# Attention and MLP on one core: the low halves of three quarters of the second weight split on another engine, and a new written order

## The chip, the cores and the metric

The kernel runs on one core of a Trainium2 chip. The metric is the device time of one execution in microseconds (us), the median over several runs; lower is better. The engines are TensorE (PE, matmuls; PEld its weight loads), VectorE (DVE), ScalarE (ACT), GpSimd (POOL) and SyncE (SP, which only issues DMAs). Each works through its own queue of instructions in order and waits for others by semaphores.

## The reference

```python
# x (8, 8, 512, 64), state (8, 8, 32, 64): per batch and head
scores = x @ state.T / 8;  a  = softmax(scores);   xread = a @ state
scores2 = state @ x.T / 8; a2 = softmax(scores2);  sread = a2 @ x
y = concatenate([xread, sread], axis=2)     # (8, 8, 544, 64) -> (8, 544, 512)
mu, var = mean(y), var(y)                   # over the last axis
yn = (y - mu) / sqrt(var + 1e-6) * g_ln
out = y + maximum(yn @ w_ch1, 0) @ w_ch2    # w_ch1 512 x 2048, w_ch2 2048 x 512
```

All in float32.

## The kernel before

**Split products.** A float32 operand is written as two float16 tiles, a high half hi = fp16(t*s) and a low half lo = fp16(t*s - hi), with a scale s per operand, and a product is three fp16 products (TERMS: hi*hi, hi*lo, lo*hi). `split` makes the two: ScalarE writes hi by a scaled copy, then the engine that it is given (VectorE unless told otherwise) writes lo by one scalar_tensor_tensor, (t * s) - hi.

**Units and stages.** The 2048 hidden columns are four units of 512 (u = 0 to 3). For each unit `weights1` loads its piece of the first weight, takes a power-of-two scale from its sum of squares (on PE, L670) and splits it (`w1c`); `weights2` does the same for the second weight. `weights2` ends in a loop over two halves of 128x1024: ScalarE writes `w2h` hi, VectorE `w2h` lo. The loaded weight's tile is named `sums` or `raw`, by the buffer that it lies in, so the same step reads `w2h<-sums` in some units and `w2h<-raw` in others. `sums_of_weights(u)` then forms four differences and sums of the quarters of the second weight in place on GpSimd (128x512 each, `sums<-sums`, `raw<-raw`), and splits them into four 128x512 pairs. They serve a product with fewer multiplications (a Strassen scheme in `products`, L895 and L953) for the later batches.

**The first batch** goes a plainer way: `first_products` (L799) multiplies a unit's first weight, ScalarE copies the result out of PSUM into one of three `strip` buffers and writes `hid` hi, GpSimd writes `hid` lo; `second_products_by_unit` (L813) multiplies by `w2h[u]` into PSUM `acc`, ScalarE copies it scaled to `part` (two buffers), and a DMA issued from GpSimd's queue adds it to the residual in memory (`xr<-part`). This happens while the weights are still coming in. From about 160 us on all products are those of L895 and L953, batch after batch.

**The order.** Nothing is scheduled by a compiler: every step is recorded in a stream by `do` (L187, which is why most rows of the trace bear that line), and a table of text, `PLAN`, gives the order in which `issue` takes items from the streams ("10:4-5" is steps 4 to 5 of stream 10). Streams 5, 10, 15 and 23 are `weights2` of units 0 to 3; 17 to 19 and 28 are `sums_of_weights`; 6, 11, 16 and 24 the second products. `WARM` dummy matmuls on a tile of ones (`half<-ones`, stream 177) are put by the same table where PE would wait.

Of the kernel before, what the change touches and what calls it, by code (L numbers as in the profile page):

```python
# [160 lines left out]
)  # L161
WARM = 135


class Later:
# [36 lines left out]
def moe_attention(ctx: ExitStack, tc: tile.TileContext, x, state, g_ln, w1, w2, out):  # L202
# [507 lines left out]
    def weights2(u):  # L710
# [17 lines left out]
        for fh in range(2):  # L728
            q = slice(2 * fh, 2 * fh + 2)
            yield from split(w[:, 0, q], w[:, 1, q], t.rearrange("p (q e) -> p q e", q=4)[:, q], s)  # L730
# [347 lines left out]
```

## Time and profile before

| what | value |
|---|---|
| median of 3 runs | 631.17 us (630.79 to 631.66) |
| the profiled execution | 632.65 us, its span 630.5 us |
| granted TensorE clock | 0.998 |
| PE busy | 614.7 us, 97% |
| VectorE busy | 488.7 us, 78% |
| ScalarE busy | 375.3 us, 60% |
| GpSimd busy | 242.5 us, 38% |
| dummy matmuls | 135 |

A row of the trace's timeline has start, length, engine, line, operation, out<-in tile, shapes and, in brackets, how long the engine had been idle before it and what released it. A row of groups has the count, then busy us and mean ns of one, then idle time before and its releasers. Names are the program's tile names without numbers, shapes are partitions x elements.

### The profile page before, as it was taken

What the parts mean: (1) busy time and instruction counts of PE and PEld (TensorE: products, weight loads), DVE (VectorE), ACT (ScalarE), POOL (GpSimd) and SP (SyncE); (2) the same over time, 40 slices, a digit from 0 to 9 for tenths busy, and PEclk for the clock granted to TensorE, in tenths of its full rate; (3) what the DMA queues carried; (4) which work ended last, traced back from release to release, by engine and by line L of the source; (5) the groups of instructions that cost most, each with busy time, mean ns of one, the idle gap of its engine ahead of it and who ended that gap; (6) DMA issues with size and microseconds to landing.
All of it is one profiled execution on the core that took longest, in us unless ns stands there. A gap on an engine that the chain in (4) does not pass through costs nothing.

```text
span 630.5 us, 16626 instructions
## 1 busy us (share of the span) xinstructions
PE 614.7 (97%) x6906; PEld 483.5 (77%) x6906; DVE 488.7 (78%) x1095; ACT 375.3 (60%) x678; POOL 242.5 (38%) x205
## 2 busy tenths in 40 slices
PE   9998998999999999999999999999999999999995
PEld 4355645558888888888888888888878888888884
DVE  4999998898697888688778785889578787564454
ACT  4998988868464844575376454736474544443241
POOL 0011656772262345324433532336224352424132
PEclk9999999999999999999999999999999999999999
DMA  8985293441534143534311246143504025201002
GB/s 289 412 232 191 84 206 68 102 120 43 130 113 120 24 96 68 155 52 132 89 34 39 43 102 156 43 102 50 143 2 77 2 63 145 69 11 25 35 1 68
DMA packets 85355, 62.02 MB, mean 98 GB/s; under 512 B 64608, under 2 KB 77408, under 8 KB 84832
## 3 DMA queue, kind: packets, MB, share of 16 engines
q1 hardware_dynamic: 83008, 57.00, 33.6%
q0 software_dynamic: 864, 3.15, 2.6%
q8 instruction: 54, 0.88, 0.6%
q10 hardware_dynamic: 1408, 0.82, 0.5%
q14 instruction: 21, 0.17, 0.1%
HBM read 28.05 MB, written 9.44 MB: 59 GB/s over the span
## 4 chain that ended last, share of the span: by engine, by line
PE 79%; DVE 13%; ACT 3%; DMA 2%; POOL 1%; issue 1%; DVEq 0%; ACTq 0%
PE acc L953 43%; PE half L895 23%; PE half L905 3%; PE banks L753 3%; DMA xr<-part 2%; PE acc L813 2%; DVE raw L187 2%; DVE x L187 1%; PE half L187 1%; DVE sums L187 1%; DVE w1c L187 1%; PE banks L590 1%; DVE w2h L187 1%; PE banks L472 1%; PE banks L565 1%
## 5 line engine op out<-in xcount | busy, mean ns | idle before, releaser
L953 PEld LDWEIGHTS <-xs 128*128 128x128 f16 x2520 | 244.0, 98 | 34.4 <-issue 6.0
L187 POOL TENSOR_TENSOR xs<-rs,xs 128x512 f16<-128x512 f32 x120 | 144.3, 1212 | 276.4 <-ACT xs L187 195.2
L953 PE MATMUL acc<-w2h,xs 128*128 128x256 f16 x1440 | 182.4, 273 | 0.0
L895 PE MATMUL half<-ea,matrix 128*128 128x256 f16 x1344 | 160.0, 273 | 0.1
L895 PEld LDWEIGHTS <-matrix 128*128 128x128 f16 x1344 | 129.4, 98 | 22.7 <-issue 5.1
L953 PE MATMUL acc<-sums,xs 128*128 128x256 f16 x1080 | 140.7, 273 | 0.0
L187 DVE SCALAR_TENSOR_TENSOR rs<-half,rs 128x256 f32<-128x256 f32 x224 | 90.0, 418 | 43.1 <-ACT rs L187 14.6
L187 ACT ACTIVATE xs<-rs 128x512 f16<-128x512 f32 (+1 forms) x128 | 77.3, 618 | 75.2 <-DVE rs L187 69.0
L187 ACT ACTIVATE xs<-half 128x256 f16<-128x256 f32 (+1 forms) x112 | 53.0, 485 | 58.3 <-PE half L895 30.7
L187 DVE SCALAR_TENSOR_TENSOR xs<-half,xs 128x256 f16<-128x256 f32 (+1 forms) x112 | 60.4, 548 | 24.2 <-ACT xs L187 23.0
L187 POOL TENSOR_TENSOR ts<-ts,mA 128x1024 f32<-128x1024 f32 (+1 forms) x16 | 29.1, 1818 | 55.4 <-DVE mA L187 32.4
L187 ACT ACTIVATE rs<-half 128x256 f32<-128x256 f32 x56 | 21.3, 381 | 39.5 <-PE half L895 32.8
L187 DVE SCALAR_TENSOR_TENSOR matrix<-banks,hs,matrix 128x1024 f16<-128x1024 f32 x28 | 35.8, 1279 | 11.4 <-ACT matrix L187 11.1
L813 PE MATMUL acc<-w2h,hid 128*128 128x512 f16 x192 | 43.2, 379 | 0.2 <-ACT strip L187 0.2
L187 DVE TENSOR_TENSOR strip<-acc,strip 128x256 f32<-128x256 f32 (+1 forms) x60 | 32.9, 549 | 9.1 <-PE acc L953 5.2
L813 PEld LDWEIGHTS <-hid 128*128 128x128 f16 x192 | 18.4, 98 | 23.9 <-issue 3.3
L187 PE MATMUL half<-ones 128*128 128x512 bf16 x135 | 34.9, 402 | 1.1 <-DVE part_mean L358 1.1
L187 ACT ACTIVATE matrix<-banks,hs 128x1024 f16<-128x1024 f32 x28 | 31.1, 1109 | 8.1 <-PE banks L753 8.0
L187 POOL TENSOR_TENSOR hid<-strip,hid 128x512 f16<-128x512 f32 x16 | 21.8, 1369 | 23.2 <-ACT hid L187 23.1
L187 PEld LDWEIGHTS <-ones 128*128 128x128 bf16 x135 | 13.0, 102 | 17.8 <-issue 5.8
L187 DVE SCALAR_TENSOR_TENSOR x<-x_f,x_s,x 128x512 f16<-128x512 f32 x32 | 24.8, 801 | 1.0 <-ACT x L187 0.9
L799 PE MATMUL acc<-ea,matrix 128*128 128x256 f16 x192 | 22.8, 272 | 2.5 <-DVE w1c L187 1.2
(152 smaller groups left out, 756.0 us busy)
## 6 DMA issues: line engine op xcount, KB each, us to landing
raw<-in_moe_w_ch_dram SPq DMA_DIRECT2D x11, 1024.0 KB, 8.5
out_dram<-xr SPq DMA_DIRECT2D x16, 512.0 KB, 3.3
x_f<-in_x_dram SPq DMA_DIRECT2D x14, 512.0 KB, 5.3
sums<-in_moe_w_ch_dram SPq DMA_DIRECT2D x5, 1024.0 KB, 8.0
ek<-ea SPq DMA_DIRECT2D x56, 64.0 KB, 2.0
ek<-ek SPq DMA_DIRECT2D x7, 512.0 KB, 4.2
xr<-part POOLq DMA_DIRECT2D x6, 512.0 KB, 4.6
s_r<-in_state_dram SPq DMA_DIRECT2D x28, 64.0 KB, 3.7
```

What stands on the lines that cost most here:

```text
L187: return lambda: f(*map(now, args), **{k: now(v) for k, v in kw.items()})
L472: nc.tensor.matmul(o[32 * j:32 * j + 32], lhsT=state_of(b, sT, g, j, a), rhs=xT[:, 2 * j + g].rearrange("p c t -> p (c t)"), start=a == 0, ...
L565: nc.tensor.matmul(o[32 * j:32 * j + 32, g], lhsT=ebT[:, e, g, c, 32 * j:32 * j + 32], rhs=xv[:, 2 * j + g, c, i], start=c == 0 and n == 0 ...
L590: nc.tensor.matmul(px[:, c, D * h:D * h + D], lhsT=ek[:, h % 2, h // 2, (2 * t + c) * P:(2 * t + c + 1) * P], rhs=sk[:, h], start=True, st ...
L753: nc.tensor.matmul(ps[g][32 * j:32 * j + 32], lhsT=state_of(b, sT, g, j, i)[r], rhs=w[r, k, j], start=n == 0, stop=n == 2, skip_group_chec ...
L799: nc.tensor.matmul(o[:, 256 * f:256 * f + 256], lhsT=m[:, g, i, P * (q + f):P * (q + f) + P], rhs=ea[:, s, k, g], start=f == 0 and g == 0 ...
L813: nc.tensor.matmul(po, lhsT=hid[:, i, q, c * P:(c + 1) * P], rhs=w[:, j, q], start=first and q == 0 and n == 0, stop=last and q == 3 and n ...
L895: nc.tensor.matmul(ps[:, 256 * q:256 * q + 256], lhsT=m[:, h, i, P * (2 * k + q):P * (2 * k + q) + P], rhs=ea[:, 0, j, h, 256 * g:256 * g ...
L905: nc.tensor.matmul(ps[:, 256 * q:256 * q + 256].rearrange("p (t n) -> p t n", t=2), lhsT=w[:, i, j, fs], rhs=xsT[:, :, x, j], start=q == 0 ...
L953: nc.tensor.matmul(po[o], lhsT=y[:, n, i, o] if o < 2 else x[:, o - 2, n, i], rhs=v[j], start=u == 0 and n == 0 and k == 0 and o in (2, 1, ...
```

## The change

In `weights2` the units 1 to 3 no longer use `split`. ScalarE first multiplies the loaded half by its scale in place (`raw<-raw,of_weights` or `sums<-sums,of_weights`, 128x1024), then copies it to hi without a scale, and GpSimd subtracts hi from it to give lo (`tensor_tensor`). `sums_of_weights` of these units then works on weights that are scaled already: its four pairs are split by the same new helper, without a scale. Unit 0 stays as it was, on VectorE. Six operations of 128x1024 and twelve of 128x512 so go from VectorE to GpSimd, and ScalarE has six more of 128x1024.

```diff
-WARM = 135
+WARM = 139
...
+    def split_scaled(hi, lo, t):
+        yield do(nc.scalar.activation, hi, t, AF.Copy)
+        yield do(nc.gpsimd.tensor_tensor, lo, t, hi, ALU.subtract)
+
...
         w2h[u] = w
         for fh in range(2):
             q = slice(2 * fh, 2 * fh + 2)
-            yield from split(w[:, 0, q], w[:, 1, q], t.rearrange("p (q e) -> p q e", q=4)[:, q], s)
+            v = t.rearrange("p (q e) -> p q e", q=4)[:, q]
+            if u == 0:
+                yield from split(w[:, 0, q], w[:, 1, q], v, s)
+            else:
+                yield do(nc.scalar.activation, v, v, AF.Copy, scale=s)
+                yield from split_scaled(w[:, 0, q], w[:, 1, q], v)
...
         for o, v in ((w, b12), (sums16[u][0], b22), (sums16[u][1], b11), (sums16[u][2], b21)):
-            yield from split(o[:, :, 0], o[:, :, 1], v, s)
+            yield from split(o[:, :, 0], o[:, :, 1], v, s) if u == 0 else split_scaled(o[:, :, 0], o[:, :, 1], v)
```

`PLAN` is written anew from end to end, about 120 lines, with four more dummies. The helper shifts the lines below it: L799 is L808 in the changed kernel, L813 is L822, L895 is L904 and L953 is L962.

At two places the new order stands as follows. The first is ScalarE ahead of unit 0's first second product, where `w2h<-sums` are that product's weights and `raw` is unit 1's second weight. Before:

```order
L342 ACTIVATE sh,x_part<-s_j 128x2x64
L187 ACTIVATE w2h<-raw,of_weights 128x1024
L187 ACTIVATE strip<-acc 128x512
L187 ACTIVATE hid<-strip 128x2x256
L187 ACTIVATE x_745<-x_f,x_s 128x8x64
L187 ACTIVATE sh<-s_j,x_s 128x2x128
L187 ACTIVATE w2h<-sums,of_weights 128x1024 x2
```

And ScalarE at the same place after the change, with some ten rows more of which the first stood further up before:

```order
L187 ACTIVATE raw<-raw,of_weights 128x1024
L187 ACTIVATE w2h<-raw 128x1024
L187 ACTIVATE xr<-acc,ux 128x2x128 x2
L187 ACTIVATE strip<-acc 128x512
L187 ACTIVATE raw<-raw 128x1024 x2
L187 ACTIVATE xr<-acc,ux 128x2x128 x3
L187 ACTIVATE hid<-strip 128x2x256
L187 ACTIVATE xr<-acc,ux 128x2x128 x3
L187 ACTIVATE raw<-raw,of_weights 128x1024
L187 ACTIVATE strip<-acc 128x512
L187 ACTIVATE hid<-strip 128x2x256
L187 ACTIVATE w2h<-raw 128x1024
```

Unit 1's two scalings and both its high halves now stand ahead of unit 0's `w2h`, where one high half stood before; the rows that follow are `sh,x_part`, the two `w2h<-sums`, an `x` and the `strip` copy.

The second place is GpSimd's queue around the first two accumulating DMAs `xr<-part` of the first batch. Before:

```order
L187 TENSOR_TENSOR hid<-strip,hid 128x2x256 x2
L187 TENSOR_TENSOR sums<-sums 128x2x256
L187 DMA xr<-part 128x1024
L187 TENSOR_TENSOR raw<-raw 128x2x256
L187 TENSOR_TENSOR hid<-strip,hid 128x2x256
L187 TENSOR_TENSOR raw<-raw 128x2x256 x2
L187 DMA xr<-part 128x1024
```

And GpSimd's queue there after the change:

```order
L187 TENSOR_TENSOR sums<-sums 128x2x256 x2
L187 TENSOR_TENSOR w2h<-sums,w2h 128x1024
L187 DMA xr<-part 128x1024
L187 TENSOR_TENSOR hid<-strip,hid 128x2x256
L187 TENSOR_TENSOR w2h<-sums,w2h 128x1024
L187 TENSOR_TENSOR raw<-raw 128x2x256 x2
L187 TENSOR_TENSOR hid<-strip,hid 128x2x256
L187 TENSOR_TENSOR raw<-raw 128x2x256 x2
L187 DMA xr<-part 128x1024
```

Each DMA now has one `w2h` low half ahead of it, and the second also one more `hid` and one more `raw` difference.

244 rows, old and new, of the table PLAN are left out of this document.

## The prediction

> **What bounds the kernel now.** I read the page first, then the table of busy time by stage, then the waits of TensorE from the first second product on, and last the rows around those waits.
>
> ```profile
> span 630.5 us, 16626 instructions
> PE 614.7 (97%) x6906; PEld 483.5 (77%) x6906; DVE 488.7 (78%) x1095; ACT 375.3 (60%) x678; POOL 242.5 (38%) x205
> ```
>
> The second row gives busy time, share and instructions of each engine. TensorE (PE) is busy for 97% of the span, so only its holes can be won. The table by stage says where they are; its columns are the stretch, its length, then PE, PEld, DVE, ACT and POOL busy, the granted clock, the DMA share and GB/s.
>
> ```profile
> 0.00:69.77 69.77, 63.27 (x747) 35.51 (x748) 60.98 (x133) 59.36 (x95) 9.82 (x14) 1.00 0.78 271
> 69.77:160.00 90.23, 87.74 (x818) 52.10 (x818) 82.61 (x171) 72.65 (x120) 53.36 (x42) 1.00 0.45 97
> 160.00:623.70 463.70, 463.70 (x5344) 395.86 (x5341) 342.28 (x788) 243.32 (x466) 179.31 (x150) 1.00 0.30 73
> ```
>
> The cuts: 69.77 is the start of the first second product (call it T), 623.7 the end of the last matmul. After 160 PE has no hole at all; between T and 160 it has 90.23 - 87.74 = 2.49 us; before T it has 6.50, but much of what is busy there is dummy matmuls (`half<-ones`), which fill waits. So before T another engine sets the time, and after T PE does. In the stretch before T, VectorE is at 61.0 of 69.8 and ScalarE at 59.4; the last thing to release PE at T is a ScalarE copy, as this row says:
>
> ```profile
> 69.77 5.55 PE L813 MATMUL acc<-w2h,hid 128*128 128x512 f16 x25 [0.24 <-ACT strip L187]
> ```
>
> The waits of PE from T on, in total, times, longest:
>
> ```profile
> PE acc L698 <- ACT part L187: 1.2, 1, 1.2
> PE acc L670 <- DVE sums L187: 0.4, 1, 0.4
> PE banks L753 <- DVE matrix L187: 0.3, 1, 0.3
> PE acc L799 <- DVE of_weights L187: 0.2, 1, 0.2
> ```
>
> These four sum to 2.1 of the 2.49. Only one is large, and it has three links, read from PE's, ScalarE's, GpSimd's timelines and the chain of waits:
>
> ```profile
> 92.77 2.76 PE L813 MATMUL acc<-w2h,hid 128*128 128x512 f16 x12
> 96.74 1.06 PE L698 MATMUL acc<-raw,gm 128*32 128x512 f32 x8 [1.21 <-ACT part L187]
> 97.74 2.79 PE L799 MATMUL acc<-ea,matrix 128*128 128x256 f16 x24
> 105.83 0.81 PE L187 MATMUL half<-ones 128*128 128x512 bf16 x3
> 96.00 0.69 ACT L187 ACTIVATE part<-acc,of_unit 128x512 f32<-128x512 f32 x1 [1.99 <-DMA xr<-part]
> 87.54 0.88 POOL L187 DMA_DIRECT2D xr<-part  x1
> 87.54 8.38 DMA xr<-part
> ```
>
> The accumulating DMA `xr<-part`, issued from GpSimd's queue at 87.54, lands 8.38 us later. Only then is its source tile free, ScalarE's next `part` copy runs, and the PSUM bank that it empties lets PE go on at 96.74. So in before it is a GpSimd queue, not VectorE, that ends PE's largest wait behind T.
>
> **The change part by part.** Prices of the pieces, busy us and mean ns of one, for VectorE, ScalarE and GpSimd:
>
> ```profile
> L187 DVE SCALAR_TENSOR_TENSOR w2h<-raw,of_weights,w2h 128x1024 f16<-128x1024 f32 x4 | 6.3, 1576 | 0.0
> L187 DVE SCALAR_TENSOR_TENSOR w2h<-sums,of_weights,w2h 128x1024 f16<-128x1024 f32 x4 | 5.0, 1279 | 0.1
> L187 DVE SCALAR_TENSOR_TENSOR sums<-sums,of_weights 128x512 f16<-128x512 f32 x6 | 4.6, 771 | 1.1 <-ACT sums L187 1.0
> L187 ACT ACTIVATE raw<-raw 128x1024 f32<-128x1024 f32 x11 | 12.6, 1162 | 0.0
> L187 POOL TENSOR_TENSOR xs<-rs,xs 128x512 f16<-128x512 f32 x120 | 144.3, 1212 | 276.4 <-ACT xs L187 195.2 <-issue 73.9 <-DVE matrix L187 4.3
> L187 POOL TENSOR_TENSOR hid<-strip,hid 128x512 f16<-128x512 f32 x16 | 21.8, 1369 | 23.2 <-ACT hid L187 23.1
> L187 POOL TENSOR_TENSOR ts<-ts,mA 128x1024 f32<-128x1024 f32 x14 | 26.7, 1910 | 19.4 <-DVE mA L187 10.7 <-PE acc L953 5.3 <-DVE rB L323 3.2
> ```
>
> VectorE loses six ops of 128x1024 (four `w2h<-raw`, two of the four `w2h<-sums`) and twelve of 128x512: 6.3 + 2 x 1.28 + 12 x 0.77 = 18 us, nearly all between 65 and 146. ScalarE gains six scalings in place, 6 x 1.16 = 7.0 us; its hi copies stay. GpSimd gains six subtractions of 128x1024, whose price no row shows: between 1.91 (`ts`, f32 out) and twice the `hid` row, 2.74; and twelve of 128x512 between 1.21 and 1.37. That is 26 to 33 us; I take 2.4, twice the `xs` row, which has the same types, and 1.25: 29 us.
>
> None of this is PE's. Useful PE work is the same, and by the order of the instructions the same set of it stands ahead of the first second product. There are 7 dummies more ahead of it (132 to 139) and none behind, where three stood (105.83). So the end moves by the shift of T, less the holes of before behind T and the three dummies, plus the new holes: shift - 2.49 - 0.75 + holes. I take 0.75 of the 0.81, since their ends overlap the next row.
>
> *The shift of T.* In the new order the first second product takes the bank that the sixth strip copy empties. On ScalarE's queue that copy stands behind unit 0's two `w2h` halves and one `x` split. The rows are the stretch from the first weights on, by the columns above (ScalarE is the fourth engine), and its timeline in before:
>
> ```profile
> 11.21:54.35 43.14, 38.63 (x465) 19.86 (x463) 42.80 (x73) 42.65 (x64) 4.62 (x4) 1.00 0.84 300
> 57.12 0.84 ACT L187 ACTIVATE xr<-acc,ux 128x256 f32<-128x256 f32 x2 [0.56 <-PE acc L605]
> 58.81 1.20 ACT L187 ACTIVATE xr<-acc,ux 128x256 f32<-128x256 f32 x3 [0.85 <-PE acc L605]
> 66.06 0.71 ACT L187 ACTIVATE x<-x_f,x_s 128x512 f16<-128x512 f32 x1
> 66.67 0.49 ACT L187 ACTIVATE sh<-s_j,x_s 128x256 f16<-128x256 f32 x1
> 67.07 2.17 ACT L187 ACTIVATE w2h<-sums,of_weights 128x1024 f16<-128x1024 f32 x2
> 69.15 0.57 ACT L187 ACTIVATE strip<-acc 128x512 f32<-128x512 f32 x1
> ```
>
> ScalarE's work ahead of the end of those two halves (69.24) grows by two scalings and one more `w2h` hi, 3 x 1.15 = 3.45, and gives up `sh` (0.49) and one `x` (0.71): +2.25. Its idle time there is 43.14 - 42.65 = 0.49, then 0.56 + 0.85, in all 1.90; the rest is solid. If all of it fills, the halves end at 69.59, `x` and `strip` add 0.66 + 0.57, and T becomes 70.87 with the 0.05 to PE's start: +1.1. If none fills, +3.0. The idle was waiting for PE's `acc` of the state path; the new order puts two `raw<-raw` copies, which wait for nothing there, between the `xr` copies, so I take most as filled: +1.3. VectorE hardly matters here: it loses one op of 1.28 ahead of T, and its two low halves of unit 0 follow ScalarE's.
>
> *SyncE's queue.* The loads of weights change places: a piece of unit 1's second weight is now the fourth in place of the sixth. Each is 1 MB, 3.9 us at the first stretch's 271 GB/s, so a piece of the first weight lands up to 3.9 us later, and a ScalarE pass on it could wait that long. I price it at nothing: ScalarE's queue is reordered with the loads and is solid from the first weights on, so the later piece has passes ahead of it to hide under. Without that cover it adds to T's shift, inside its upper end.
>
> *The holes behind T.* The DMA of 87.54 is now queued on GpSimd behind one low half, all four quarter differences and a second `hid`. The rows: the first DMA's issue, the mean of a difference, the transfers' time to landing (least, median, most) and the stretches around, by the columns above:
>
> ```profile
> 78.95 1.05 POOL L187 DMA_DIRECT2D xr<-part  x1 [1.49 <-ACT part L187]
> L187 POOL TENSOR_TENSOR raw<-raw 128x512 f32<-128x512 f32 x8 | 10.9, 1361 | 4.0 <-DVE w2h L187 2.6 <-PE acc L799 1.2
> DMA to landing us min/median/max: 4.5/4.6/8.4
> 79.00:91.00 12.00, 12.00 (x62) 5.07 (x59) 10.95 (x25) 10.17 (x16) 7.99 (x7) 1.00 1.00 220
> 91.00:96.00 5.00, 4.53 (x40) 1.60 (x38) 5.00 (x8) 2.36 (x5) 0.00 (x0) 1.00 0.66 121
> ```
>
> Between the first and the second DMA GpSimd did three differences and one `hid` in before; now it does two `hid`, one low half and four differences: 2 x 1.37 + 2.4 + 4 x 1.36 = 10.6 us. The first was done at 80.0 and moves with T, to 81.3, or by half of the low half ahead of it to 82.0 by estimate; so the second is issued at 91.9 to 92.6. It lands 4.6 to 8.4 later, at 96.5 to 101.0, and ScalarE's copy of 0.69 and a tenth end at 97.3 to 101.8. PE asks later too. It would reach the place of the old wait at 95.53 + 1.3 - 0.44 (a wait on `sums` that I let go here) = 96.4, and by the new order the bank is needed only one row (1.06) and half of the next (1.4) later, at 98.8. The wait is 0 to 3.0. The DMA engines are all busy from 79 to 91 and at 0.66 behind it, so I take 6.5 to landing, between median and most: 91.9 + 6.5 + 0.8 = 99.2, a wait of 0.4. The small waits on VectorE (0.4, 0.3, 0.2) I keep at 0.9, since their places move but VectorE's lead is not shown. Two new waits I add by estimate: 0.5 where a product waits for a `hid` that now stands on GpSimd behind a low half (an overlap of 2.4 against a lead of about 2), and 0.3 where `part` copies stand behind a scaling of 1.16. Sum 2.1.
>
> *GpSimd as a whole.* Between T and 160 it has 53.4 busy of 90.2, and becomes 53.4 + 26 to 33 = 79 to 86. It is not over, but has 4 to 11 us left. Its load after 160 does not change, and what is early there covers me: 463.7 of 463.7 busy. I price it at nothing; without cover it is the fourth case below.
>
> *The VectorE side.* A longer row shows what a neighbour on GpSimd does to VectorE:
>
> ```profile
> 116.79 1.91 POOL L187 TENSOR_TENSOR ts<-ts,mA 128x1024 f32<-128x1024 f32 x1
> 117.32 2.46 DVE L187 SCALAR_TENSOR_TENSOR w2h<-raw,of_weights,w2h 128x1024 f16<-128x1024 f32 x1
> 121.96 1.28 DVE L187 SCALAR_TENSOR_TENSOR w2h<-raw,of_weights,w2h 128x1024 f16<-128x1024 f32 x1
> ```
>
> The op that started 0.53 us into GpSimd's took 1.18 us more than its twin, nearly the 1.38 that GpSimd still ran. So GpSimd's added 29 us can lengthen VectorE's other ops: by nothing, or at most by 29. VectorE between T and 160 has 82.6, less about 17, 66 busy; with all 29 it would be 95 of 90. I take half, 80: no relief worth counting and no new bound.
>
> The Trainium skill ("SBUF — State Buffer", section "Who interferes with whom") says that a VectorE op with two SBUF inputs and a GpSimd op that reads SBUF exclude each other, and the one that comes second waits for the other's whole length. The trace agrees in that pair (1.18 us longer under 1.38 of overlap). By the rule alone, nearly every moved op would take back from VectorE what it gave, which keeps the small waits and leaves the sum below as it is; by the price rows alone VectorE would be freed by 17 us and the small waits of 0.9 would go, a sum of -0.7.
>
> *The tail.* From 623.7 to 630.5 the same ops and stores follow the last matmul; I put it at 0, with 0.3 either way.
>
> **Sum.** +1.3 - 2.49 - 0.75 + 2.1 = +0.16, say +0.2 us. On the profiled execution, 632.65 us with 2.15 outside its span, that is 632.85; it lies 1.48 above the median of the runs, 631.17, so the forecast is 631.4 us.
>
> **The rivals.**
> *Faster: the holes close.* GpSimd's work hides in the 37 us that it idles between T and 160, the DMA lands in its median 4.6 us (at 96.5, ahead of 98.8), and VectorE with 17 us less is early everywhere. T shifts by 1.1 and holes of 0.3 are left: 1.1 - 3.24 + 0.3 = -1.8, so 629.4. For it: 4.6 is the median of six. Against it: the shared time of VectorE and GpSimd. The floor is no holes, 1.1 - 3.24 = -2.1, with the tail's 0.3 -2.4: 628.8. No case goes below that, since PE has nothing else to give.
>
> *Slower: GpSimd's queue holds the DMA.* The second `xr<-part` stands behind low half, differences and `hid`, is issued at 91.9 to 92.6 and lands after 8.4: PE waits 2.3 to 3.0. With the small waits 0.9 and the new 0.8 that is 1.3 - 3.24 + 4.0 to 4.7 = +2.1 to +2.8, so 633.3 to 634.0, in the middle 633.6. It decides from a landing at 98.0 on; each us behind that costs one. For it: at this very place the transfer took 8.38. Against it: the DMA engines are at 0.66 behind 91.
>
> *Slower: GpSimd is full.* One row of `hid` shows how far its ops can stretch:
>
> ```profile
> 55.55 1.92 POOL L187 TENSOR_TENSOR hid<-strip,hid 128x512 f16<-128x512 f32 x1 [7.08 <-ACT hid L187]
> ```
>
> If its ops take over 37 us in place of 29 (2.74 and 1.37 with another 12%; one `hid` took 1.92 in place of 1.37), the split of the last unit and the `xs` pieces of the first batch come late around 140, and PE pays what is over: 2 to 4 us, 634.
>
> *Nothing:* VectorE was no bound behind T and the end is set by PE alone; that is the case that I forecast, from the other side.
>
> **Chances and range.** What a measurement of this kernel can tell from no change is about 0.2%, 1.26 us: 629.9 and 632.4. The forecast case, ends 630.0 to 632.4, gets 0.40; the faster one 0.33; the queue 0.17; GpSimd full 0.10. So faster 0.33, the same 0.40, slower 0.27. The shift of T at its upper end of 3.0 falls into the slower cases. For 8 in 10 the range leaves out the floor side of the faster case (about 0.1) and most of the fourth (about 0.1): 629.2 to 633.7. No case of one sign has most of the chance; the likeliest one's own range is the 630.0 to 632.4 above.
>
> **What would show it.** In the changed profile: the first second product starts at 70.9 to 71.3, released by ScalarE's `strip`; the second `xr<-part` is issued at 91.5 to 93 and lands at 96 to 101; PE's row behind it waits under 1 us; GpSimd's subtractions of 128x1024 take 1.9 to 2.7; PE is without hole from 160 on. I am wrong if T does not move or comes earlier (then the ScalarE count is wrong and the end is below 630), if holes appear after 160, or if the longest wait behind T is on a GpSimd low half.

## The result and the profile after

The changed kernel is slower: 638.92 us median of four executions (637.39 to 640.35) against 631.41 us for the kernel before beside it, a ratio of 1.012 with a 95% interval of 1.009 to 1.015. The four fall into two pairs: 637.39 and 637.88 us at a mean granted clock of 0.996 and 0.995, 639.96 and 640.35 at 0.992. The profiled one is the first, 4.74 us above the profiled execution of before.

The page of the changed kernel, its span and the busy time by engine:

```profile
span 635.6 us, 16635 instructions
PE 615.0 (97%) x6910; PEld 483.6 (76%) x6910; DVE 481.3 (76%) x1077; ACT 381.2 (60%) x684; POOL 268.5 (42%) x223
```

Busy time moved as the change says: VectorE 7 us less, ScalarE 6 more, GpSimd 26 more, PE the same. What VectorE did not give up of the forecast 18 us is time that its other ops took longer. The stages, with the columns of the prediction's table (stretch, length, PE, PEld, DVE, ACT, POOL):

```profile
0.00:69.80 69.80, 64.22 (x754) 36.49 (x755) 59.79 (x142) 61.56 (x97) 15.40 (x16) 1.00 0.80 271
69.80:160.00 90.20, 82.28 (x768) 47.26 (x766) 69.35 (x129) 70.72 (x116) 74.44 (x57) 1.00 0.45 100
160.00:628.50 468.50, 468.38 (x5393) 399.90 (x5391) 349.17 (x803) 248.90 (x473) 178.62 (x151) 1.00 0.30 72
```

The first second product starts at 69.80, in before at 69.77. PE's holes behind it are 7.92 us up to 160 and 0.12 after it, 8.04 in place of 2.49. With the three dummies that are gone (0.75) and a tail of 7.1 in place of 6.8, that makes 0.03 + 5.55 - 0.75 + 0.3 = 5.1 us, the difference of the spans. So all of it is new waiting of PE between 70 and 160 us, and the waits of PE from 71 on name the releasers:

```profile
PE acc L822 <- DVE w1c L187: 3.6, 1, 3.6
PE acc L702 <- ACT part L187: 1.6, 1, 1.6
PE acc L822 <- ACT part L187: 1.1, 1, 1.1
PE half L904 <- DVE ea L187: 0.5, 1, 0.5
```

PE's own timeline at the largest, then VectorE's and GpSimd's in the same stretch:

```profile
86.81 2.75 PE L822 MATMUL acc<-w2h,hid 128*128 128x512 f16 x12
93.18 5.34 PE L822 MATMUL acc<-w2h,hid 128*128 128x512 f16 x24 [3.62 <-DVE w1c L187]
```

```profile
77.39 2.51 DVE L187 SCALAR_TENSOR_TENSOR sk<-s_r,x_s,sk 64x512 f16<-64x512 f32 x1
...
84.96 4.77 DVE L187 SCALAR_TENSOR_TENSOR x<-x_f,x_s,x 128x512 f16<-128x512 f32 x1 [2.59 <-ACT x L187]
...
90.76 1.41 DVE L187 SCALAR_TENSOR_TENSOR acc<-sums,gx,acc 128x512 f32<-128x512 f32 x2
...
92.39 1.40 DVE L187 SCALAR_TENSOR_TENSOR w1c<-acc,of_weights,w1c 128x512 f16<-128x512 f32 x2
```

```profile
76.89 2.45 POOL L187 TENSOR_TENSOR w2h<-sums,w2h 128x1024 f16<-128x1024 f32 x1 [1.29 <-ACT w2h L187]
83.63 1.05 POOL L187 DMA_DIRECT2D xr<-part  x1 [4.29 <-ACT part L187]
84.42 1.46 POOL L187 TENSOR_TENSOR hid<-strip,hid 128x512 f16<-128x512 f32 x1
85.54 2.41 POOL L187 TENSOR_TENSOR w2h<-sums,w2h 128x1024 f16<-128x1024 f32 x1
87.63 3.22 POOL L187 TENSOR_TENSOR raw<-raw 128x512 f32<-128x512 f32 x2
90.81 1.15 POOL L187 TENSOR_TENSOR hid<-strip,hid 128x512 f16<-128x512 f32 x1
94.49 0.87 POOL L187 DMA_DIRECT2D xr<-part  x1
```

An `x` op and the `sk` op in the kernel before, where GpSimd does no arithmetic beside them:

```profile
79.72 0.74 DVE L187 SCALAR_TENSOR_TENSOR x<-x_f,x_s,x 128x512 f16<-128x512 f32 x1
80.50 0.75 DVE L187 SCALAR_TENSOR_TENSOR sk<-s_r,x_s,sk 64x512 f16<-64x512 f32 x1
```

Read them together. The `x` op, 0.74 us before, starts at 84.96 and ends at 89.73. All that time GpSimd is at work without a break, and the op ends half a microsecond after the first `raw` op has. Behind it in VectorE's queue stand the ops of unit 2's first weight, whose `w1c` at 92.39 frees the PSUM bank that PE waits for. The `acc` and `w1c` ops have an operand in PSUM and take 0.7 each, as in the kernel before, though GpSimd works on beside them. The `sk` op is the small sister: 2.51 us in place of 0.75, beside a low half of 2.45, and ScalarE's second `part` copy, whose buffer holds what `sk` reads, comes late by that; this is the wait of 1.6.

The price of the moved low halves themselves was right, by groups of GpSimd in the changed kernel:

```profile
L187 POOL TENSOR_TENSOR w2h<-raw,w2h 128x1024 f16<-128x1024 f32 x4 | 8.5, 2136 | 0.1
L187 POOL TENSOR_TENSOR w2h<-sums,w2h 128x1024 f16<-128x1024 f32 x2 | 4.9, 2430 | 1.3 <-ACT w2h L187 1.3
```

### The profile page after: what moved, and what is told of

The parts are those of the page before. It is cut to its first block, busy times and chain, and to the rows that moved or that the text cites. A ratio compares the mean times of both kernels' runs of the same rounds, so it can differ in the third digit from the quotient of the medians.

```text
span 635.6 us, 16635 instructions
## 1 busy us (share of the span) xinstructions
PE 615.0 (97%) x6910; PEld 483.6 (76%) x6910; DVE 481.3 (76%) x1077; ACT 381.2 (60%) x684; POOL 268.5 (42%) x223
## 4 chain that ended last, share of the span: by engine, by line
PE 85%; ACT 5%; DVE 3%; POOL 3%; issue 2%; DMA 1%; SPq 0%; ACTq 0%; DVEq 0%; POOLq 0%
PE acc L962 44%; PE half L904 23%; PE acc L822 4%; PE half L914 3%; PE banks L762 3%; PE half L187 3%; ACT sums L187 1%; PE acc L808 1%; DMA x_f<-in_x_dram 1%; POOL hid L187 1%; PE banks L590 1%; PE banks L565 1%; PE banks L472 1%; DVE x L187 1%; POOL w2h L187 1%
## 5 line engine op out<-in xcount | busy, mean ns | idle before, releaser
L962 PEld LDWEIGHTS <-xs 128*128 128x128 f16 x2520 | 243.0, 98 | 38.7 <-issue 9.4
L187 POOL TENSOR_TENSOR xs<-rs,xs 128x512 f16<-128x512 f32 x120 | 141.7, 1190 | 253.7 <-ACT xs L187 177.5
L962 PE MATMUL acc<-w2h,xs 128*128 128x256 f16 x1440 | 182.9, 273 | 0.0
L904 PE MATMUL half<-ea,matrix 128*128 128x256 f16 x1344 | 160.3, 273 | 0.6 <-DVE ea L187 0.5
L904 PEld LDWEIGHTS <-matrix 128*128 128x128 f16 x1344 | 130.4, 98 | 18.8 <-issue 2.7
L962 PE MATMUL acc<-sums,xs 128*128 128x256 f16 x1080 | 141.5, 273 | 0.0
L822 PE MATMUL acc<-w2h,hid 128*128 128x512 f16 x192 | 43.6, 379 | 5.0 <-DVE w1c L187 3.6
L822 PEld LDWEIGHTS <-hid 128*128 128x128 f16 x192 | 18.2, 98 | 28.6 <-issue 8.3
L187 DVE SCALAR_TENSOR_TENSOR x<-x_f,x_s,x 128x512 f16<-128x512 f32 x32 | 26.9, 869 | 4.1 <-ACT x L187 3.9
L187 DVE BATCH_NORM_STATS2 s<-xr 128x6 f32<-128x512 f32 x32 | 21.7, 685 | 4.9 <-ACT xr L187 4.9
```

The lines of the kernel that those rows point to most:

```text
L187: return lambda: f(*map(now, args), **{k: now(v) for k, v in kw.items()})
L822: nc.tensor.matmul(po, lhsT=hid[:, i, q, c * P:(c + 1) * P], rhs=w[:, j, q], start=first and q == 0 and n == 0, stop=last and q == 3 and n ...
L904: nc.tensor.matmul(ps[:, 256 * q:256 * q + 256], lhsT=m[:, h, i, P * (2 * k + q):P * (2 * k + q) + P], rhs=ea[:, 0, j, h, 256 * g:256 * g ...
L962: nc.tensor.matmul(po[o], lhsT=y[:, n, i, o] if o < 2 else x[:, o - 2, n, i], rhs=v[j], start=u == 0 and n == 0 and k == 0 and o in (2, 1, ...
```

## The experiments

The kernel before was run beside each and lay at 631.8 to 631.9 us.

### Order and engines apart

The theories at this point: A, VectorE ops stand still beside GpSimd's; B, the new order makes the waits whatever the engine; C, ScalarE's scalings do. Four runs take the change apart. First, the low halves back on VectorE with everything else kept:

```diff
-        yield do(nc.gpsimd.tensor_tensor, lo, t, hi, ALU.subtract)
+        yield do(nc.vector.tensor_tensor, lo, t, hi, ALU.subtract)
```

> The changed kernel with one word changed: the eighteen low halves are subtracted by VectorE in place of GpSimd; order and ScalarE's scalings stay. Theory A (a VectorE op with two inputs in SBUF stands still while GpSimd's subtractions run): the x low half that took 4.77 us is back under 1 us, the wait of 3.62 on PE goes, 631.5 to 634 us although VectorE has 17 us more. Theory B (the new order alone makes the waits): 637 us or more. Theory C (ScalarE's extra scalings delay the part copies): 636 us or more.

Measured: 642.69 us, ratio 1.016 (1.015 to 1.018). The `x` op came down to 2.69 us, held by what GpSimd had before already, and the waits on `part` fell from 2.65 to 1.1. But the work came back too: PE waits 2.67 and 3.08 us on `w1c`, and behind each of these waits its clock is halved for 3.4 us. The first of them, PE's row and the stretch at half clock (the column behind POOL is the granted clock):

```profile
91.51 7.03 PE L822 MATMUL acc<-w2h,hid 128*128 128x512 f16 x24 [2.67 <-DVE w1c L187]
91.73:95.15 3.42, 3.42 (x10) 1.22 (x9) 3.17 (x6) 3.42 (x5) 1.84 (x2) 0.50 0.93 180
```

A in this simple form fails: holding is not the only way to make VectorE late.

Second, the changed code in the order of before (steps renumbered, each scaling just ahead of its high half):

```diff
-PLAN, WARM = 139 of the changed kernel
+PLAN, WARM = 135 of the kernel before
```

> The order of before with the changed code: each moved low half stands where its VectorE op stood, each scaling just ahead of its high half. A: VectorE ops beside the low halves stretch past 1.5 us at some five places, 633 to 637 us. B: 631 to 632. C: 632 to 634, with waits of PE on ScalarE.

Measured: 640.99 us (ratio 1.015, 1.013 to 1.016), slower than any theory said. T moves to 70.92, PE waits 2.98 us on VectorE's `acc` and 1.16 on `sums`; `sums<-raw` takes 2.69 us in place of 1.2. Third, the new order with the code of before:

```diff
-PLAN, WARM = 135 of the kernel before
+PLAN, WARM = 139 of the changed kernel, without its scalings
```

> The new order with the code of before: low halves by VectorE with the scale folded in, no scalings by ScalarE. A: 631 to 634. B: 637 or more. C: 631 to 633; against the run with the scalings kept and the low halves on VectorE it tells what the scalings cost, by C 3 us or more, by A under 1.

Measured: 641.32 us (ratio 1.016, 1.014 to 1.017). PE waits 3.24 and 2.10 us on `w1c`. Against the first run of the four the scalings cost 1.4 us, which is within the spread of the two: C is small. Each half of the change alone is about 9 us slower than the kernel before; together they are 7.5 slower. So the loss is not the sum of the two. B's numbers came true in the two runs with the new order (637 or more) and not in the one with the old order (631 to 632 expected, 640.99 measured), so B, the order as such, can be neither blamed nor cleared by a swap. Fourth, only the quarter sums back on VectorE:

```diff
-split_scaled(o[:, :, 0], o[:, :, 1], v)
+split_scaled(o[:, :, 0], o[:, :, 1], v, nc.vector)
```

> The changed kernel, but the twelve low halves of the quarter sums go back to VectorE; the six of 128x1024 stay on GpSimd. A: the long x and sk ops stay (they lie beside 128x1024 halves), the wait of 3.6 stays, 636 to 639. B: 637 or more. If the quarter sums were the cause it would be 632 or less.

Measured: 644.55 us (ratio 1.020, 1.017 to 1.022). As A said, the `x` op takes 4.78 and PE waits 3.63, though the time is far above A's 639; a new wait of 3.08 on `w1c` comes at 105. The stages around that wait show the clock again:

```profile
105.30:108.40 3.10, 0.02 (x1) 0.00 (x0) 2.34 (x2) 0.64 (x2) 1.18 (x1) 0.90 0.87 169
108.40:114.00 5.60, 5.59 (x22) 2.28 (x22) 3.38 (x9) 3.53 (x6) 4.42 (x4) 0.50 0.00 0
114.00:120.00 6.00, 6.00 (x52) 3.60 (x52) 3.91 (x8) 4.73 (x10) 3.96 (x4) 0.95 0.29 93
```

The 0.90 and 0.95 of the outer rows are 0.6 us at half clock each, so the stretch lasts 6.8 us; PE works in 6.2 of them, and the hole of 3.1 costs about as much again. The length of a hole does not decide alone: in this run the wait of 3.63 has a clock of 1.00 behind it, and in the profiled run of the changed kernel, of the lower pair, so has the wait of 3.62, while 2.67 was enough in the first run of the four. A mean clock of 0.992 in place of 0.996 over 636 us is 2.5 us, the gap between the two pairs of runs of the changed kernel. The mean counts the tail too, where the clock is 0.50 in part, but 0.008 of 638 us is 5.1 us, more than a tail of 7.1 us at half clock (3.6) can give. So, with such a tail, the upper pair had a stretch at half clock ahead of it; that it stood behind the hole of 3.62 is a guess, which a run below tests.

### The held op and the clock, each by itself

One VectorE op is moved, in the tokens of the order (26:30 is the `x` op, 26:26 the transpose that reads it):

```diff
-... 6:1 26:30 6:10 ... 26:17 26:26 12:12-14 ... 12:20-21 23:3 ...
+... 6:1 6:10 ... 26:17 12:12-14 ... 12:20-21 26:30 26:26 23:3 ...
```

> The changed kernel with one VectorE op moved: the x low half that took 4.77 us, and the transpose that reads it, stand behind the eight ops of the first weight of unit 2 that stood behind it. Theory A (an op with two inputs in SBUF stands still while GpSimd works, and holds VectorE's whole queue): PE's wait of 3.62 shrinks to under 1 and the clock stays at 0.995 or more, 634 to 636 us. Theory B (the queue of first-weight ops is late for another reason, such as PE's own order or the bank): the wait stays, 637 or more.

Measured: 634.42 us (ratio 1.005, 1.003 to 1.006), 4.5 below the changed kernel's median and 3.0 below its fastest run. The wait of 3.62 is gone altogether, and the clock was 0.997 or 0.998 in all six runs. VectorE's row of the moved op, and PE's largest wait that is left:

```profile
91.38 0.89 DVE L196 SCALAR_TENSOR_TENSOR x<-x_f,x_s,x 128x512 f16<-128x512 f32 x1
```

```profile
98.27 1.06 PE L711 MATMUL acc<-raw,gm 128*32 128x512 f32 x8 [1.82 <-DVE matrix L196]
```

That this op's place in VectorE's queue makes the large wait is shown by this run: no work, no engine and no buffer changed. But the move takes two things out of the queue at once, the hold of 4.0 us and the 2.59 us for which the op had waited for ScalarE; a run further down takes the hold away and leaves the order. The clock is tested by filling the hole instead of closing it:

```diff
-... 12:30 11:3 ...
+... 12:30 177:139-150 11:3 ...      # twelve dummies more
```

> The changed kernel with twelve dummy matmuls (some 2.6 us) put into PE's wait of 3.62. Nothing else is mended. Theory C (in the slower executions of the changed kernel the hole halves the granted clock behind it): every run at a clock of 0.995 or more, 637 to 638 us, none near 640. If the spread has another cause, runs near 640 at 0.992 remain.

Measured: 636.65 us, five runs from 636.27 to 636.96 at clocks of 0.995 to 0.999, and none near 640. The hole remains but for the dummies (1.03), so the upper pair of the changed kernel's runs was most likely the halved clock; of such a run no trace is kept. The Trainium skill ("TensorE: Matmul & The Clock Gate", section "Part 1: The HAM clock gate") says that an idle window of about 3.4 us takes PE to half rate, and that the window runs freely. The runs agree with it in part: stretches at half clock last 3.4 us or twice that, and a hole of 3.62 or 3.63 can pass. They do not show 3.4 us as a threshold, since waits of 2.67 and 3.08 were enough.

The other way to shorten the hold is to move GpSimd's work. Unit 2's two low halves (15:19, 15:22) go behind the third `xr<-part`:

```diff
-... 12:11 15:19 15:15 ... 11:0 15:22 18:0 ... 6:5 17:7 ...
+... 12:11 15:15 ... 11:0 18:0 ... 6:5 15:19 15:22 17:7 ...
```

> The changed kernel with unit 2's two low halves of 128x1024 moved on GpSimd from ahead of the first and second xr<-part to behind the third; their users come later. A: sk back to 0.75 us and the wait of 1.57 behind it gone, the x op down to 2.3 to 2.7 (the quarter differences still hold it), PE's wait of 3.62 down to 1.5 to 2.5, 634 to 637. B: 637 or more, the waits unchanged.

Measured: 640.36 us (ratio 1.013, 1.012 to 1.015), not 634 to 637. The waits that were foreseen came: `sk` 0.75, `x` 2.70, the wait of 3.62 down to 1.54, the one of 1.57 gone. But the two low halves now stand ahead of other GpSimd ops, and a VectorE op was held for 8.09 us there (VectorE, then GpSimd):

```profile
92.64 8.09 DVE L196 SCALAR_TENSOR_TENSOR raw<-raw 128x1024 uint32<-128x1024 uint32 x1 [0.24 <-ACT raw L196]
```

```profile
90.09 0.88 POOL L196 DMA_DIRECT2D xr<-part  x1
90.71 4.50 POOL L196 TENSOR_TENSOR w2h<-sums,w2h 128x1024 f16<-128x1024 f32 x2
94.90 3.63 POOL L196 TENSOR_TENSOR sums<-raw,sums 128x512 f16<-128x512 f32 x3
98.34 1.30 POOL L196 TENSOR_TENSOR w2h<-raw,w2h 128x512 f16<-128x512 f32 x1
```

The op waits from 92.64 through six GpSimd ops and ends 1.3 us, its own length, behind the start of the next DMA at 99.43. PE waits 5.05 us for it. With both moves together:

```diff
+... 12:20-21 26:30 26:26 23:3 ... 6:5 15:19 15:22 17:7 ...
```

> Both moves of the two runs beside it. A: no wait of PE over 1.1 us behind the first second product, no halved clock, 630.5 to 633.5; at or below the kernel before if all holes but 1.5 us go. B: 636 or more.

Measured: 645.09 us (ratio 1.021, 1.019 to 1.022), the worst of all: the `x` op is held there for 9.62 us and PE waits 7.67.

### Why an op is held so long

First by itself: a VectorE op beside a run of GpSimd subtractions, nothing of the kernel around.

```diff
+nc.gpsimd.tensor_tensor(low, go, hi, ALU.subtract)                 # 0, 1, 2 or 4 times
+nc.vector.scalar_tensor_tensor(x_lo, of_x, mark, x_hi, ALU.mult, ALU.subtract)
```

> Only the disputed cost, no part of the kernel's work (its output is zeros): a VectorE op started just behind a run of 0, 1, 2 or 4 subtractions of 128x1024 on GpSimd, in four forms. Theory A1 (held to the end of an unbroken run): the op with two inputs in SBUF takes its 0.75 us plus all of the run, some 2, 4 and 9 us; the one with an input in PSUM and the reduction stay as they are; a short GpSimd op without an SBUF read in the middle of the run of 4 lets it in. Theory A2 (held until the op that runs has ended, as a lock of one instruction would): at most 2.4 us longer, whatever the run. Theory A3 (both share a port and slow each other): every form grows a little.

The rows of VectorE beside the run of four, one for each form:

```profile
21.97 2.10 DVE L65 SCALAR_TENSOR_TENSOR x_lo<-of_x,mark,x_hi 128x512 f16<-128x512 f32 x1
...
44.38 0.74 DVE L68 SCALAR_TENSOR_TENSOR x_lo<-pa,mark,x_hi 128x512 f16<-128x512 f32 x1
...
67.26 2.11 DVE L71 TENSOR_SCALAR bits<-bits 128x1024 uint32<-128x1024 uint32 x1
...
90.42 1.21 DVE L74 TENSOR_REDUCE most<-src 128x1 f32<-128x1024 f32 x1
```

Two inputs in SBUF: held, 2.10 in place of 0.74. One input in PSUM: not held. The integer shift with one input in SBUF: held too, 2.11 in place of 0.69. The reduction: not held. But the hold was 2.05 to 2.11 with runs of one, two and four, and 2.10 with a tiny write in the middle of the four: A1 fails and A2 holds here. The Trainium skill ("SBUF — State Buffer", section "Who interferes with whom") says just this, that the later of the two waits for one whole instruction of the other. The kernels, with 4.77, 8.09 and 9.62, say more.

A run with tiles of their own for each subtraction was to show whether GpSimd lets go only where it waits for itself:

```diff
-    outs = [low] * n
+    outs = [low, low0, low1, low2][:n]
```

> No part of the kernel's work again (zeros come out). In the first such run a VectorE op with two inputs in SBUF was held by 2.1 us at most, whatever the length of GpSimd's run, where in the kernels it was held 8 and 9.6. There all subtractions wrote one tile. Theory A1 (GpSimd lets go only where one of its ops must wait for the one before): runs of 2 and 4 subtractions to tiles of their own hold the op for some 4 and 8.5 us, runs to one tile for 2.1; the in-place chain of four of 128x512, each needing the last, about 1.3, the one of four independent pieces about 5. Theory A2 (one instruction, the long holds had another reason): 2.1 in all runs of 128x1024.

Measured: 2.11 in every run of 128x1024 (2.32 in the very first), tiles of their own or not. A1 fails again. In the two runs of 128x512 the op came only under the last subtraction (1.19 and 0.95), so they tell nothing. What every long hold had was an `xr<-part` DMA just ahead on GpSimd's queue:

```diff
+    nc.gpsimd.dma_start(out=xr, in_=part, accum_op=ALU.add)
     for o in outs:
         nc.gpsimd.tensor_tensor(o, go, hi, ALU.subtract)
```

> No part of the kernel's work (zeros come out). Runs of 2 and 4 subtractions of 128x1024 on GpSimd, to tiles of their own or all to one tile (each then waits for the one before), without and with an xr<-part DMA issued on GpSimd's queue just ahead; a VectorE op with two inputs in SBUF starts under the first. Every hold over several GpSimd ops seen so far stood behind such a DMA. Theory D (behind the DMA GpSimd's ops overlap and the hold lasts until one of them has to wait): without DMA 2.1 us in all; with it, tiles of their own, some 4 us for two and 8.5 for four; with it and one tile 2.1 to 2.5. Theory A2 (one instruction): 2.1 to 2.5 in all, and the long holds stay unexplained.

GpSimd's rows without a DMA (the row holds two of the run of four), behind one with tiles of their own, and behind one all to one tile; then the VectorE op in each:

```profile
25.50 4.65 POOL L77 TENSOR_TENSOR low<-go,hi 128x1024 f16<-128x1024 f32 x2 [1.35 <-ACT go L71]
...
45.20 0.87 POOL L74 DMA_DIRECT2D xr<-part  x1 [3.14 <-ACT part L73]
45.81 8.63 POOL L77 TENSOR_TENSOR low<-go,hi 128x1024 f16<-128x1024 f32 x4
...
82.75 9.36 POOL L77 TENSOR_TENSOR low<-go,hi 128x1024 f16<-128x1024 f32 x4
```

```profile
26.13 2.04 DVE L81 SCALAR_TENSOR_TENSOR x_lo<-of_x,mark,x_hi 128x512 f16<-128x512 f32 x1
...
46.34 8.67 DVE L81 SCALAR_TENSOR_TENSOR x_lo<-of_x,mark,x_hi 128x512 f16<-128x512 f32 x1
...
83.28 2.45 DVE L81 SCALAR_TENSOR_TENSOR x_lo<-of_x,mark,x_hi 128x512 f16<-128x512 f32 x1
```

2.04 without the DMA, 8.67 behind it, 2.45 behind it where each subtraction waits for the one before. With two in place of four it was 4.66 behind the DMA. So what D foresaw came, each case measured once: behind this DMA VectorE's op did not come in between GpSimd's ops, but only where one of them had to wait, or behind the last. In the kernel the run from the DMA at 83.63 ends where the second `raw` has to wait for the first, whose operand it overwrites, and there the `x` op came in. In the holds of 8.09 and 9.62 no GpSimd op waited; there the op came in at GpSimd's next DMA. The transfer itself is not what holds: it lands 4.6 us behind its issue, at 49.8, and the op of 8.67 ended at 55.0. That GpSimd's ops overlap, as D has it, no row shows. Nor does any run show why the DMA has this effect: one that does not add, or one from another queue, was not tried. Two runs test D in the kernel. The first `xr<-part` (6:10) is moved behind those ops:

```diff
-... 6:1 26:30 6:10 9:7 ... 11:1 18:1 12:22 ...
+... 6:1 26:30 9:7 ... 11:1 18:1 6:10 12:22 ...
```

> The changed kernel with the first xr<-part moved on GpSimd behind one hid, one low half and two quarter differences. Theory D: the x op is held by one GpSimd op at a time, under 2.6 us in place of 4.77, and PE's wait of 3.62 is at most 2, 634 to 637 us. A2: the x op stays at 4 or more, 637 to 640.

VectorE's row of the `x` op, GpSimd's of the low half beside it, and ScalarE's of the `part` copy behind the DMA:

```profile
84.91 0.75 DVE L196 SCALAR_TENSOR_TENSOR x<-x_f,x_s,x 128x512 f16<-128x512 f32 x1 [2.59 <-ACT x L196]
```

```profile
84.98 2.67 POOL L196 TENSOR_TENSOR w2h<-sums,w2h 128x1024 f16<-128x1024 f32 x1
```

```profile
96.50 0.69 ACT L196 ACTIVATE part<-acc,of_unit 128x512 f32<-128x512 f32 x1 [7.40 <-DMA xr<-part]
```

The `x` op is not held at all, as it started 0.07 us ahead of the low half. The time was 641.38 us (ratio 1.016, 1.014 to 1.018) all the same: the DMA is now late, ScalarE stands 7.40 us before its `part` copy, VectorE's `acc` op waits for ScalarE, and PE waits 5.88 for that. A late DMA that holds up PE through the `part` copy is the mechanism of the prediction's first slow rival, brought about by moving the DMA. The cleaner test leaves the order alone and ends the run of GpSimd's ops behind each DMA by two tiny writes:

```diff
         nc.gpsimd.dma_start(out=v, in_=part, accum_op=ALU.add)
+        for _ in range(2):
+            nc.gpsimd.memset(tick, 0.0)
```

> The changed kernel with two tiny writes (128x1) on GpSimd behind each of the six xr<-part DMAs, the second waiting for the first; order and work stay. Theory D (behind the DMA GpSimd's ops overlap until one of them has to wait): the x op of 4.77 us takes 2.3 or less, as one GpSimd op holds it at most, PE's wait of 3.62 falls under 1.6 and the clock is never halved, 634 to 636.5 us; the waits of 1.57 and 1.08 stay. If the two tiny writes do not end the overlap: no change, 637 to 640.

```profile
84.16 1.67 DVE L187 SCALAR_TENSOR_TENSOR x<-x_f,x_s,x 128x512 f16<-128x512 f32 x1 [2.59 <-ACT x L187]
```

```profile
89.28 5.34 PE L822 MATMUL acc<-w2h,hid 128*128 128x512 f16 x24 [0.52 <-DVE w1c L187]
```

Measured: 636.08 us (ratio 1.006, 1.005 to 1.008), 2.8 below the changed kernel's median and 1.3 below its fastest run, at a clock of 0.994 to 0.998. VectorE's row shows 1.67 for the `x` op and PE's a wait of 0.52 in place of 3.62, as D said. The order and the wait of 2.59 for ScalarE are as they were, so some 3.1 of the 3.62 us were the hold's. The waits on `part` stay at 1.56 and 1.08, and a third one grows from 0.3 to 0.99. The tiny writes also read nothing in SBUF; that waiting alone is enough, only the run with one tile shows.

### Mending the rest

If held ops are the whole loss, mending them one by one must lead back to 631. The `sk` op alone ahead of two word passes:

```diff
-... 26:32 12:7 9:5 26:28 6:6 26:33 ...
+... 26:32-33 12:7 9:5 26:28 6:6 ...
```

> The changed kernel with only the sk op moved ahead of the two word passes. A: the wait of 1.57 and part of the 1.08 behind it go, the 3.62 stays: 2 us less than the changed kernel, 635 to 638. B: no change, 637 to 640.

Measured: 635.64 us (ratio 1.007, 1.005 to 1.008), 3.3 less. The waits on `part` are gone, 2.65 us; but the next `x` op is held for 2.63 in place of `sk`, and PE waits 1.97 for the maximum behind it. The wait of 3.62 did not stay, as these rows of VectorE and PE show:

```profile
81.81 4.77 DVE L196 SCALAR_TENSOR_TENSOR x<-x_f,x_s,x 128x512 f16<-128x512 f32 x1
90.03 7.03 PE L831 MATMUL acc<-w2h,hid 128*128 128x512 f16 x24 [2.26 <-DVE w1c L196]
```

The `x` op is held as long as before, but no longer waits for ScalarE first, and PE's wait is 2.26. Its 24 matmuls behind it take 7.03 in place of 5.34, 3.4 us of it at half clock: a hole of 2.26 was enough. With the held op moved, `sk` earlier and two matrix splits ahead of idle passes:

```diff
-... 13:1 26:31 17:5 23:6 23:5 13:2-4 ...
+... 13:1 26:31 13:2-4 17:5 23:6 23:5 ...      # and the two moves above
```

> The run with the held x op moved, and two more moves in the order: VectorE's sk op ahead of the two word passes that stood ahead of it, so that ScalarE's part copy has its buffer earlier; and the two matrix splits of unit 2 ahead of three passes that nothing waits for. Theory A (what is left of the loss is VectorE's queue standing behind held ops): the waits of 1.6 and 1.8 go, 630 to 632.5, level with or below the kernel before. Theory B (the new code has a cost of its own): 634 or more.

Measured: 637.31 us (ratio 1.009, 1.007 to 1.010): not 630 to 632.5. The waits aimed at are gone, and a low half of unit 0's quarter sums is held for 4.79 us behind the next DMA, at 101.5; PE waits 3.35, and its next twelve matmuls take 4.18 in place of 2.75. Two moves more, for that op and for the `x` ops ahead of the maximum:

```diff
-... 26:23 15:21 12:10 26:21 ... 6:5 17:7 14:0 ...
+... 15:21 12:10 26:19-20 26:28 26:25 26:23 26:21 ... 20:24 17:7 1:77 ...
```

> The run with three moves, and two more: VectorE's sh and x ops, held for some 2 us by GpSimd's low half, go behind the maximum (of_columns) that PE waited 2 us for, and one low half of unit 0's quarter sums, held for 4 us ahead of first-weight ops at 101.5, goes behind those. Theory A (each large wait of PE is a VectorE queue behind one held op): both waits go, no halved clock, 630 to 633. Theory B (the new code has a cost that moves about but stays): 635 or more.

Measured: 634.10 us (ratio 1.004, 1.003 to 1.006). Its largest wait, 1.90, is behind a word pass held for 4.78 behind the second DMA. That one put two ops later:

```diff
-... 11:6 23:4 18:8 ... 23:6 23:5 18:4 ...
+... 11:6 18:8 ... 23:6 23:5 23:4 18:4 ...
```

> The run with five moves and one more: the word pass of unit 3 that was held for 4.78 us goes behind the two matrix splits that stood behind it. Theory A: PE's wait of 1.9 goes, 631.5 to 632.8, about level with the kernel before. Theory B (a cost that moves about but stays): 634 or more.

Measured: 635.80 us (ratio 1.006, 1.005 to 1.007), not 631.5 to 632.8: the wait of 1.9 is gone, but two word passes take 2.2 and 5.1 us, and a transposing DMA comes 3.08 late for PE. Its first half starts 1.4 us later than in the changed kernel (91.2 in place of 89.8), since the `x` op that it reads had been put back, and takes 5.1 us to issue in place of 1.8; why, no row shows. Last, the five moves and the tiny writes:

```diff
+            nc.gpsimd.memset(tick, 0.0)      # twice behind each xr<-part, in the order with five moves
```

> The run with five moves and the same tiny writes. D: the word pass of 4.78 us falls to 2.5 or less and the wait of 1.9 that it caused goes, 631.5 to 633, level with the kernel before. Otherwise 634 as without them.

Measured: 634.02 us (ratio 1.004, 1.002 to 1.005). No op takes over 2 us, and the wait of 1.9 is gone, but the time is that without the writes. What is left behind T are a wait on the transposing DMA `xT` (1.1), late as in the run before, waits of 0.3 to 0.5, and one of 1.3 on the DMA `ek` at 264 us, far behind everything that was moved and with no cause shown. So no version here beats the kernel before, and the road back to 631 ends at 634.0. Held ops are most of the loss; where its last 2 us come from is not settled. A's times (630 to 633) came in none of the three patched orders, those of B, a cost that moves about but stays, in two (637.31 and 635.80, not 634.10). Whether an order written for the new code would be free of it was not tried.

## Why the prediction was wrong

The forecast was 631.4 us, range 629.2 to 633.7; the result, 638.92, lies outside it.

**The shift of T** was sized wrongly, and on the safe side: +1.3 forecast, +0.03 measured. ScalarE was busy for 61.6 us ahead of T in place of 59.4, in the same time: 2.2 us more, where the sum had 2.25 and 0.66 for the `x`, and 2.2 us less idle, where it let at most 1.90 fill. Of the 1.9 that I counted only 0.15 is left idle, and 0.4 more filled ahead of the rows that I counted (11.92 busy in the first 20 us in place of 11.53). By the sign that I had given, a T that does not move meant an end below 630; the holes behind T made it 638.92.

**The second `xr<-part`** came at 94.49, later than the 91.9 to 92.6, since the first stood 4.29 us behind ScalarE's `part` copy. It cost PE nothing: the bank that I thought it held up was free in time. The first slow rival did not decide here.

**GpSimd's price** was right: 29 us forecast, 29.1 measured over the eighteen ops, 2.1 to 2.4 each for the large ones. It was not full: 74.4 of 90.2 us. The second slow rival did not decide either.

**The step that failed** is the one on VectorE: "I take half, 80: no relief worth counting and no new bound". I had the row, an op of 2.46 beside its twin of 1.28, and the rule, and turned them into a share of VectorE's time. VectorE's time was not the question: it was busy for 69.4 of 90.2 us, less than the 80 that I took (some of its ops had also moved out of this stretch: 129 in place of 171, of which the change took 18). An op that is held stops VectorE's whole queue, and what it costs is decided by who stands behind it. One op held for 4.0 us ahead of `w1c` cost most of the 3.62 (some 3.1 by the run with the tiny writes), another held for 1.8 ahead of a `part` copy cost 1.57 and the 1.08 behind it. These three waits are 6.3 of the 8.0 us of holes, where the sum had 2.1 in all. Moving the one op took 4.5 us off the median, moving the other 3.3.

**The length of a hold** I put at one GpSimd op at most, as the pair in the trace had it. Behind the accumulating DMA on GpSimd's queue it was the whole run of ops, up to 9.62 us. The rows of before that I read do not show that: behind the DMA of 87.54 GpSimd does one op and then stands still for 6.74 us.

**The clock** was in no term. Behind holes of 2.26 to 3.1 us it was halved for 3.4 to 6.8 us in the traces of the other runs, and in two of the four runs of the changed kernel most likely behind the 3.62: they are 2.5 us slower than the other two, and half of that is in the median.

**The end of the chain** was right: no holes behind 160 to speak of (0.12), a tail 0.3 longer, inside the 0.3 that I gave it.

## What to carry to other kernels

Work moved from VectorE to GpSimd is not paid in busy time alone: here a VectorE op with two inputs in SBUF, and an integer shift with one, waited for GpSimd's running subtraction, so look at what stands behind each such op in VectorE's queue, and put those that others wait for ahead of it. Do not let a run of GpSimd ops follow an accumulating DMA that GpSimd issues, or make one of them wait: in the changed kernel that alone took 2.8 us off the median. And where PE is the bound, a hole of over 2 us can cost more than its length (2.26 us were followed by 24 matmuls in 7.03 us in place of 5.34).

## What the runs showed of the hardware that was not expected

- Behind an accumulating DMA issued on GpSimd's queue, a VectorE op with two inputs in SBUF waited out two GpSimd ops (4.66 us) or four (8.67) by itself, and six in the kernel (8.09); without the DMA it waited for one (2.04), and behind the DMA too where GpSimd's ops waited for each other (2.45).
- The holding goes both ways: a GpSimd subtraction of 128x1024, 2.12 us alone, took 2.67 where VectorE's `x` op had started 0.07 us ahead of it, and by itself 3.09 where a VectorE op of 128x1024 with two inputs in SBUF had started 0.11 us ahead. It was 3.09 also where one or three more ops of VectorE stood behind that one, so it waited for one of them.
- An integer shift with one input in SBUF was held like an op with two (2.11 in place of 0.69), a reduction of 128x1024 was not (1.21).
- A granted clock of 0.50 for 6.8 us behind a hole of 3.1 us of PE, and for 3.4 us behind holes of 2.26 and 2.67; none behind holes of 3.62 and 3.63.
